# Linear attention with a GeGLU branch on one core: x and v blocks loaded in turn, the gate column made on TensorE, k steps between the weight folds, and the wq transposes released by v

## The chip, the cores and the metric

The kernel runs on one core of one Trainium2 chip. The metric is the device time of one execution in microseconds (us). One execution in each series is profiled; "span" is the length of that execution in its trace, about 2 us below the metric. On one core a run is called "slow" or "fast" by its distance from the fastest run.

## The reference

`x` is 2048 x 640. There are 32 heads of 20 columns. Everything is bf16 with f32 accumulation.

```python
g   = sigmoid((x * gate_w).sum(-1, keepdims=True))
q, k, v = split_heads(x @ wqkv)                       # wqkv 640 x 1920
pq, pk  = q @ w_phi[h], k @ w_phi[h]                  # per head, 20 x 20
phi_q   = concat(softmax(pq), softmax(-pq));  phi_k likewise
kv, z   = phi_k^T v, sum(phi_k)
o       = (phi_q kv) / (phi_q z + 1e-6)
b       = (gelu(x @ w_gate) * (x @ w_up)) @ w_down    # 640 -> 1728 -> 640
out     = g * (o @ wo) + (1 - g) * b
```

## The kernel before

The per-head product with `w_phi` is folded into the weights: `wk2 = wk . blockdiag(w_phi)` and `wq2` likewise, 640 x 640 each. So the kernel needs `wk^T` and `wq^T`: the first by TensorE transposes of the loaded `wk_raw`, the second by six transposing DMAs. Operations are issued in program order on each engine (`pe`, `act`, `dve`, `pool`) and each DMA on a queue (`sp` or `act`). A helper adds a semaphore wait for every hazard, also for a PSUM bank that is still to be read. There are eight banks; numbers such as `(6, 7)` are banks, and `"a"` or `"d"` says whether ACT or DVE moves the result from PSUM to SBUF (evicts it). In the code below, a tile is 128 rows of `x`; `k_early` makes the k product of one tile and its exponentials (exps) on ACT (`Ek`), `k_norm` normalises them on DVE, `pq` is a product with `wq2` and its exps (`Eq`), and `gram` is the product `phi_k^T v`.

The loads, in the order of issue:

```python
        xload(0, "sp"); xload(2, "act"); xload(1, "sp"); xload(3, "act")    # 128 x 640 each
        for kt in range(KD):                                                # five v blocks
            sc.dma("sp", ... self.wvk[:, kt, 0:D] <- w3[:, kt, 2 * D:3 * D], writes=[("wv", kt)])
        sc.dma("act", ... wphi_sb <- w_phi, "h d f -> d h f", writes=["wphi"])
        sc.dma("sp", ... wk_raw <- w3[:, :, D:2 * D], writes=["wk_raw"])    # 640 x 640 at once
        sc.dma("sp", gload, writes=["wgate"])                               # gate_w as a column
        for g, (h0, nh) in enumerate(self.GH):                              # six transposing DMAs
            sc.dma("sp", lambda e: e.dma_start_transpose(self.wqT[:, g, :], self.wqkv[:, h0*DH:h0*DH+P]),
                   reads=["wk_raw"] if g == 0 else [], writes=[("wqT", g)])
        xblock(1); xblock(2); xblock(3)      # transposing DMAs of the rest of x
        # ... the FFN weights follow
```

One fold makes one 128-row block of `wk2` or `wq2` from six groups of heads. It needs two banks and all six groups of the transposed weight:

```python
    def fold(self, kt, which, banks, ekey):
        for g, (h0, nh) in enumerate(self.GH):
            pe.matmul(bank(banks[h0 // 16])[...], wT[0:rows, g, kt*P:(kt+1)*P], self.BD[...], start=True, stop=True)
        # one eviction of both banks, by DVE or ACT, into wvk[:, kt, D:2D] or wq2[:, kt, :]
```

The order up to the steady loop (the part that the change rewrites):

```python
        for i in range(self.NWARM):                       # 7 matmuls of zeros
            pe.matmul(self.bank(3), self.zero[:, 0:P], self.zero[:, :])
        for t, ek in enumerate("adad"):
            self.x_transpose(t, 4 + t, ek)                # x tiles 0..3 on TensorE
        self.v_first({(1, 3): [lambda: self.blockdiag((6, 7))],      # v of four tiles, kt outermost
                      (4, 0): [ve([0], "a")],
                      (4, 1): [tk(0, 6, "d"), ve([1], "a")],         # tk: wk transposes of one group
                      (4, 2): [tk(1, 7, "d"), ve([2], "a")]})        # ve: eviction of v
        self.w_transposes("k", (2, 3, 4, 5), (0, 6, 7, 0), "dadd")
        # ... evictions of v
        for kt, (bk, ek) in enumerate(zip((6, 1, 4, 6, 0), "adada")):
            self.fold(kt, "k", (bk, bk + 1), ek)
        self.k_early(0, 2)                                # k tile 0: banks 2, 3; then its exps on ACT
        self.k_early(1, 4)
        self.fold(0, "q", (6, 7), "d")
        self.fold(1, "q", (0, 1), "a")
        self.k_early(2, 2)
        self.fold(2, "q", (6, 7), "d")
        self.fold(3, "q", (0, 1), "a")
        self.fold(4, "q", (6, 7), "d")
        self.k_norm(0)
        self.k_early(3, 4)
        self.k_norm(1)
        self.pq(0, 1, 1); self.pq(0, 0, 0); self.pq(0, 3, 3)
        self.gram(0)
        self.k_norm(2); self.pq(0, 2, 2); self.k_norm(3)
        for t in range(4, NT):                            # the steady loop
            self.vk(t)
            # ... k_norm, pq, gram; then the FFN and the output
```

The softmax here doesn't subtract the row's maximum and nothing guards it: scores larger than these inputs give would overflow.

## Time and profile before

| | before |
|---|---|
| time, median of 3 first runs | 307.3 us (306.21 to 307.35) |
| span of the profiled run | 304.7 us |
| TensorE busy | 298.0 us, 98% |
| first 512-column matmul of the steady loop | 30.97 us |
| from there to the start of the last matmul | 270.5 us |

The first two fences are from the page of the kernel before: busy time by engine, TensorE's row of the busy tenths over 40 slices, and the chain that ended last: the last instruction, followed back at each step to what released it.

```profile
PE 298.0 (98%) x2011; PEld 175.3 (58%) x2011; DVE 160.0 (53%) x312; ACT 106.8 (35%) x189; POOL 29.8 (10%) x59
...
PE   7998999999999999999999999999999999999996
```

```profile
PE 94%; DMA 2%; ACT 1%; DVE 1%; issue 0%; SPq 0%; ACTq 0%; DVEq 0%
```

TensorE is the bound, and what is left lies at the start. The chain in order of time (start, length, what) for the kernel before:

```profile
1.72 5.08 DMA wvk<-in_A_wqkv_dram
...
13.62 0.85 PE ps L327 x15
...
14.49 0.49 DVE wkT L334
...
14.99 0.50 DVE wkT L334
...
15.53 0.37 PE ps L345 x4
...
15.90 0.74 ACT wvk L360
...
18.14 2.41 PE ps L365 x17
20.55 0.61 PE ps L345 x12
21.16 1.37 PE ps L365 x10
...
27.09 0.99 ACT Eq L494 x2
...
28.12 1.25 PE ps L488 x5
```

The chain begins with the first v block (landed 6.80), passes the last two evictions of `wkT` (last one done at 15.49), the folds and k tiles 0 and 1 (until 20.55), the first two q folds, k tile 2, and ends its gaps with the eviction before pq(0,3) at 28.12. After that it is TensorE without a break.

### The profile page before, as it was taken

The page shows a single profiled execution, that of the slowest core. Times are in us where ns is not written, and L with a number is a line of the kernel's source. Part 1 is how long each engine was busy: PE and PEld are TensorE (multiplying, and loading weights), DVE is VectorE, ACT ScalarE, POOL GpSimd, SP SyncE. Part 2 cuts the span into 40 slices and gives each one's busy share as a digit, 9 for nine tenths or more (in the row PEclk, how much of TensorE's full clock was granted, in tenths as well). Part 3 has the DMA queues.
Part 4 walks back from the last instruction along what each step waited for, and adds up shares of the span by engine and source line. Part 5 has one row for each costly group of instructions (what it writes and reads, how often), then busy time and mean ns, then how long its engine had stood idle before and what let it go on. Part 6 is the DMA issues. An engine that isn't in the chain of part 4 may idle for free.

```text
span 304.7 us, 5022 instructions
## 1 busy us (share of the span) xinstructions
PE 298.0 (98%) x2011; PEld 175.3 (58%) x2011; DVE 160.0 (53%) x312; ACT 106.8 (35%) x189; POOL 29.8 (10%) x59
## 2 busy tenths in 40 slices
PE   7998999999999999999999999999999999999996
PEld 4664565655555555677545567754457764545763
DVE  1438999586775877234367710435770044567000
ACT  3388666667674222111322211123221122222111
POOL 7100000000000011111011000101110010111000
PEclk9999999999999999999999999999999999999999
DMA  7589996000000011120120111011111001110401
GB/s 222 140 150 209 369 369 221 0 2 0 2 0 0 2 22 24 24 65 25 43 20 4 22 24 43 24 43 23 17 6 44 24 26 41 22 22 0 45 22 45
DMA packets 34641, 18.29 MB, mean 60 GB/s; under 512 B 25850, under 2 KB 34618, under 8 KB 34618
## 3 DMA queue, kind: packets, MB, share of 16 engines
q1 hardware_dynamic: 33680, 17.62, 22.8%
q10 hardware_dynamic: 938, 0.35, 0.4%
q8 instruction: 16, 0.26, 0.4%
q14 instruction: 7, 0.06, 0.1%
HBM read 9.78 MB, written 2.62 MB: 41 GB/s over the span
## 4 chain that ended last, share of the span: by engine, by line
PE 94%; DMA 2%; ACT 1%; DVE 1%; issue 0%; SPq 0%; ACTq 0%; DVEq 0%
PE ps L572 37%; PE ps L654 20%; PE ps L365 12%; PE ps L660 7%; PE ps L488 6%; PE ps L609 4%; PE ps L462 4%; PE ps L376 2%; DMA wvk<-in_A_wqkv_dram 2%; PE ps L582 1%; PE ps L345 1%; ACT Eq L494 1%; PE ps L327 0%; ACT Ek L423 0%; DVE wkT L334 0%
## 5 line engine op out<-in xcount | busy, mean ns | idle before, releaser
L572 PE MATMUL ps<-xT,wu_sb 128*128 128x512 bf16 x260 | 64.6, 379 | 0.2 <-ACT Eq L494 0.2
L572 PE MATMUL ps<-xT,wg_sb 128*128 128x512 bf16 x260 | 64.6, 379 | 0.0
L654 PE MATMUL ps<-wd_sb,hT 128*128 128x320 bf16 (+2 forms) x448 | 63.8, 299 | 0.0
L575 ACT ACTIVATE gl<-ps 128x512 bf16<-128x512 f32 x52 | 31.1, 597 | 83.2 <-PE ps L572 81.0
L577 DVE TENSOR_TENSOR hT<-ps,gl 128x512 bf16<-128x512 f32 x52 | 35.7, 688 | 42.9 <-PE ps L572 42.9
L654 PEld LDWEIGHTS ps<-wd_sb,hT 128*128 128x128 bf16 x448 | 43.1, 98 | 18.2 <-DVE hT L577 0.4
L572 PEld LDWEIGHTS ps<-xT,wu_sb 128*128 128x128 bf16 x260 | 25.4, 98 | 31.1 <-issue 0.7
L365 PE MATMUL ps<-wvk,xT 128*128 128x512 bf16 (+2 forms) x220 | 40.6, 335 | 0.2 <-DVE wvk L358 0.2
L572 PEld LDWEIGHTS ps<-xT,wg_sb 128*128 128x128 bf16 x260 | 24.9, 98 | 26.9
L670 ACT ACTIVATE outsb<-ps,Gm 128x640 bf16<-128x640 f32 (+2 forms) x17 | 13.0, 763 | 74.1 <-PE ps L660 74.1
L638 POOL TENSOR_TENSOR Og<-O_59,O_60 128x640 bf16<-128x640 bf16 x16 | 22.3, 1396 | 167.8 <-DVE O_60 L636 167.8
L365 PEld LDWEIGHTS ps<-wvk,xT 128*128 128x128 bf16 x220 | 21.1, 97 | 19.5 <-DVE wvk L358 0.6
L434 DVE TENSOR_REDUCE Dk<-Ek 128x64 f32<-128x1280 bf16 x16 | 23.7, 1482 | 10.0 <-ACT gcol L426 10.0
L625 DVE RECIPROCAL RH<-ps 128x32 f32<-128x32 f32 x16 | 5.7, 358 | 43.9 <-PE ps L609 42.8
L443 DVE TENSOR_TENSOR Ek<-Ek,Dk 128x640 bf16<-128x640 bf16 x32 | 25.0, 822 | 0.5
L488 PE MATMUL ps<-xT,wq_50 128*128 128x512 bf16 x100 | 24.7, 378 | 0.3 <-ACT Eq L494 0.3
L660 PE MATMUL ps<-wo_sb,goT 128*128 128x320 bf16 (+2 forms) x160 | 24.5, 299 | 0.0
L494 ACT ACTIVATE Eq<-ps 128x512 bf16<-128x512 f32 x40 | 21.8, 607 | 5.4 <-PE ps L488 5.4
L423 ACT ACTIVATE Ek<-ps 128x640 bf16<-128x640 f32 x32 | 20.7, 703 | 2.2 <-PE ps L365 2.2
L660 PEld LDWEIGHTS ps<-wo_sb,goT 128*128 128x128 bf16 x160 | 15.5, 98 | 6.3
L609 PEld LDWEIGHTS ps<-KV,Eq 128*128 128x128 bf16 x192 | 12.0, 98 | 3.1
L609 PE MATMUL ps<-KV,Eq 128*128 128x154 bf16 x192 | 13.7, 221 | 0.0
(68 smaller groups left out, 178.7 us busy)
## 6 DMA issues: line engine op xcount, KB each, us to landing
out_dram<-outsb SPq DMA_DIRECT2D x15, 160.0 KB, 1.8
wd_sb<-in_B_w_down_dram SPq DMA_DIRECT2D x1, 2080.0 KB, 12.7
wg_sb<-in_B_w_gate_dram SPq DMA_DIRECT2D x1, 1120.0 KB, 7.0
wu_sb<-in_B_w_up_dram SPq DMA_DIRECT2D x1, 1120.0 KB, 9.5
wg_sb<-in_B_w_gate_dram SPq DMA_DIRECT2D x1, 960.0 KB, 9.0
wu_sb<-in_B_w_up_dram SPq DMA_DIRECT2D x1, 960.0 KB, 9.4
wvk<-in_A_wqkv_dram SPq DMA_DIRECT2D x5, 160.0 KB, 4.8
wk_raw<-in_A_wqkv_dram SPq DMA_DIRECT2D x1, 800.0 KB, 6.5
```

What stands on the lines that cost most here:

```text
L365: sc.op("pe", lambda e, kt=kt: e.matmul(self.bank(bank)[:, bcol:bcol + n], self.xT[:, kt, t * P:(t + 1) * P], self.wvk[:, kt, c0:c0 + n], ...
L434: sc.op("dve", lambda e: e.tensor_reduce(self.Dk[:, se, 0, :].rearrange("p (s h) -> p s h", h=H), self.Ek[:, se, :, :].rearrange("p s (h d ...
L443: sc.op("dve", lambda e, v=v, r=r: e.tensor_tensor(v, v, r, ALU.mult), reads=[("Rk", se)], writes=[("Ek", se, s)])
L488: sc.op("pe", lambda e, kt=kt: e.matmul(self.bank(bank), self.wq2[:, kt, i * P:(i + 1) * P], self.xT[:, kt, b * self.BT:(b + 1) * self.BT] ...
L494: sc.op("act", lambda e, s=s, scale=scale: e.activation(self.Eq[:, s, i, b * self.BT:(b + 1) * self.BT], self.bank(bank), AF.Exp, scale=sc ...
L572: sc.op("pe", lambda e, kt=kt, w=w, bk=bk: e.matmul(self.bank(bk), w[:, kt, c * P:(c + 1) * P], xs(kt), start=(kt == 0), stop=(kt == self. ...
L575: sc.op("act", lambda e: e.activation(self.gl[:, slot, :], self.bank(banks[0]), AF.Gelu_apprx_tanh), reads=[("ps", banks[0])], writes=[("g ...
L577: sc.op("dve", lambda e: e.tensor_tensor(self.hT[:, c, :], self.bank(banks[1]), self.gl[:, slot, :], ALU.mult), reads=[("ps", banks[1]), ( ...
L609: sc.op("pe", lambda e, s=s, i=i, n=n, o0=o0, k0=k0, bk=bk, r=r: e.matmul(self.bank(bk)[:, o0:o0 + n], self.Eq[:, s, i, t * P:(t + 1) * P] ...
L638: sc.op("pool", lambda e: e.tensor_tensor(self.Og[:, sl, :], self.O1[:, sl, :], self.O2[:, sl, :], ALU.add), reads=[("O", 0, sl), ("O", 1, ...
L654: sc.op("pe", lambda e: e.matmul(self.bank(bk, w), self.hT[:, c, tt * P:(tt + 1) * P], self.wd_sb[:, c, w0:w0 + w], start=(c == 0), stop=F ...
L660: sc.op("pe", lambda e: e.matmul(self.bank(bk, w), self.goT[:, gs, k, :], self.wo_sb[:, k, w0:w0 + w], start=False, stop=(k == self.KD - 1 ...
```

## The change

Its intent is to let TensorE work earlier and to leave it fewer gaps: x and v blocks come in turn, so v steps start before all of x is there; the gate column, a load of 640 single elements, is replaced by a row load and five small matmuls; the k steps of tiles 0 and 1 fill the time in which the folds are evicted; and the wq transposes are issued when v is loaded. The core of the diff, cuts marked:

```diff
-        xload(0, "sp")
-        xload(2, "act")
-        xload(1, "sp")
-        xload(3, "act")
-        for kt in range(KD):
-            sc.dma("sp", lambda e, kt=kt: e.dma_start(self.wvk[:, kt, 0:D], ...), writes=[("wv", kt)])
-        sc.dma("act", ... wphi ...)
+        sc.dma("act", ... self.gw_row[0:1, :] <- gate_w as one row, writes=["gw_row"])
+        for i in range(4):
+            xload(i)            # all on "sp"
+            vload(i)
+        sc.dma("sp", ... wphi ...)
+        vload(4)
         sc.dma("sp", ... wk_raw ...)
-            sc.dma("sp", gload, writes=["wgate"])
         for g, (h0, nh) in enumerate(self.GH):
             sc.dma("sp", ... dma_start_transpose(self.wqT[:, g, :], ...),
-                    reads=["wk_raw"] if g == 0 else [], writes=[("wqT", g)])
+                    reads=[("wv", 4)] if g == 0 else [], writes=[("wqT", g)])
 ...
-        for i in range(self.NWARM):  # 7
-        # four x transposes, v with kt outermost, block diagonal after (kt 1, tile 3)
+        warm(4)
+        self.gate_column(5)     # five 1x128 by 1x1 matmuls, one small copy on DVE
+        warm(1)
+        xt(0, 6, "a")
+        warm(1)
+        xt(1, 7, "d")
+        vs(0, 0); vs(0, 1); vs(1, 0); vs(1, 1)      # v_step(tile, kt)
+        xt(2, 6, "a")
+        vs(0, 2); vs(1, 2)
+        xt(3, 7, "d")
+        # ... the other v steps, block diagonal after vs(2, 0..2), wk transposes as before
-        for kt, (bk, ek) in enumerate(zip((6, 1, 4, 6, 0), "adada")):
-            self.fold(kt, "k", (bk, bk + 1), ek)
-        self.k_early(0, 2)
-        self.k_early(1, 4)
+        self.fold(0, "k", (6, 7), "d")
+        self.fold(1, "k", (4, 5), "a")
+        ks(0, 0); ks(1, 0)                          # k_step(tile, kt); tile t in banks 2t, 2t + 1
+        self.fold(2, "k", (6, 7), "d")
+        ks(0, 1); ks(1, 1)
+        self.fold(3, "k", (4, 5), "a")
+        self.fold(4, "k", (6, 7), "d")
+        ks(0, 2); ks(1, 2); ks(0, 3); ks(1, 3)
+        for t in (0, 1):
+            ks(t, 4)
+            self.k_evac(t, 2 * t)
         self.fold(0, "q", (6, 7), "d")
-        self.fold(1, "q", (0, 1), "a")
-        self.k_early(2, 2)
+        self.fold(1, "q", (4, 5), "d")
+        self.k_early(2, 0)
         self.fold(2, "q", (6, 7), "d")
-        self.fold(3, "q", (0, 1), "a")
-        self.fold(4, "q", (6, 7), "d")
+        self.fold(3, "q", (4, 5), "d")
+        self.fold(4, "q", (6, 7), "a")
         self.k_norm(0)
-        self.k_early(3, 4)
+        self.k_early(3, 2)
```

More of the change, by code (lines that the diff above doesn't have):

```diff
@@ L157, in alloc @@
         self.zero = T("zero", [P, 512], BF16)
+        self.gw_row = T("gw_row", [1, D], BF16)
+        self.one = T("one", [1, 1], BF16)
         self.gcol = T("gcol", [P, NT], F32)
@@ L191, in alloc @@
             [("xtok", [P, self.TB, D], BF16), ("wk_raw", [P, KD, D], BF16),
-             ("wkT", [P, 6, D], BF16), ("wqT", [P, 6, D], BF16), ("wq_raw", [P, KD, D], BF16)],
+             ("wkT", [P, 6, D], BF16), ("wqT", [P, 6, D], BF16)],
             [("goT", [P, 6, KD, P], BF16), ("O1", [P, 2, D], BF16), ("O2", [P, 2, D], BF16),
@@ L208, in loads @@
         w3 = self.wqkv.rearrange("(kt p) n -> p kt n", p=P)
-        def gload(e):
-            with nc.allow_non_contiguous_dma(reason="gate_w as a column"):
-                return e.dma_start(self.wvk[:, :, 2 * D:2 * D + 1], self.gw.rearrange("(kt p o) -> p kt o", p=P, o=1))
-        def xload(t, q):
-            sc.dma(q, lambda e: e.dma_start(self.xtok[:, t, :], self.x[t * P:(t + 1) * P, :]), writes=[("xtok", t)])
-        xload(0, "sp")
-        xload(2, "act")
-        xload(1, "sp")
-        xload(3, "act")
@@ L219, in loads, with xload @@
-        for kt in range(KD):
-            sc.dma("sp", lambda e, kt=kt: e.dma_start(self.wvk[:, kt, 0:D], w3[:, kt, 2 * D:3 * D]), writes=[("wv", kt)])
-        sc.dma("act", lambda e: e.dma_start(self.wphi_sb[:, :].rearrange("d (h f) -> d h f", f=DH),
-                                            self.wphi.rearrange("h d f -> d h f")), writes=["wphi"])
-        sc.dma("sp", lambda e: e.dma_start(self.wk_raw[:, :, :], w3[:, :, D:2 * D]), writes=["wk_raw"])
-        if self.QDMA:
-            sc.dma("sp", gload, writes=["wgate"])
-            for g, (h0, nh) in enumerate(self.GH):
-                sc.dma("sp", lambda e, g=g, h0=h0: e.dma_start_transpose(
-                    self.wqT[:, g, :], self.wqkv[:, h0 * DH:h0 * DH + P]),
-                    reads=["wk_raw"] if g == 0 else [], writes=[("wqT", g)])
-        else:
-            sc.dma("sp", lambda e: e.dma_start(self.wq_raw[:, :, :], w3[:, :, 0:D]), writes=["wq_raw"])
-            sc.dma("sp", gload, writes=["wgate"])
+        def xload(t):
+            sc.dma("sp", lambda e: e.dma_start(self.xtok[:, t, :], self.x[t * P:(t + 1) * P, :]), writes=[("xtok", t)])
@@ new lines, in vload @@
+        def vload(kt):
+            sc.dma("sp", lambda e: e.dma_start(self.wvk[:, kt, 0:D], w3[:, kt, 2 * D:3 * D]), writes=[("wv", kt)])
+        sc.dma("act", lambda e: e.dma_start(self.gw_row[0:1, :], self.gw.rearrange("(o n) -> o n", o=1)), writes=["gw_row"])
+        for i in range(4):
+            xload(i)
+            vload(i)
+        sc.dma("sp", lambda e: e.dma_start(self.wphi_sb[:, :].rearrange("d (h f) -> d h f", f=DH),
+                                           self.wphi.rearrange("h d f -> d h f")), writes=["wphi"])
@@ L234, in xblock @@
+        vload(4)
+        sc.dma("sp", lambda e: e.dma_start(self.wk_raw[:, :, :], w3[:, :, D:2 * D]), writes=["wk_raw"])
+        for g, (h0, nh) in enumerate(self.GH):
+            sc.dma("sp", lambda e, g=g, h0=h0: e.dma_start_transpose(
+                self.wqT[:, g, :], self.wqkv[:, h0 * DH:h0 * DH + P]),
+                reads=[("wv", 4)] if g == 0 else [], writes=[("wqT", g)])
         def xblock(b, after=()):
@@ L237, in xblock @@
                 reads=after, writes=[("xT", t) for t in range(b * 4, b * 4 + 4)])
-        xblock(1, [] if self.QDMA else ["wq_raw"])
+        xblock(1)
         xblock(2)
@@ L317, in blockdiag, with wk_transposes @@
             reads=rd, writes=["BD"])
-    def w_transposes(self, which, gs, banks, ekeys):
+    def wk_transposes(self, gs, banks, ekeys):
         sc = self.sc
-        raw, T = (self.wk_raw, self.wkT) if which == "k" else (self.wq_raw, self.wqT)
         for g, b, ek in zip(gs, banks, ekeys):
@@ L327, in w_transposes, with gate_column @@
                 sc.op("pe", lambda e, kt=kt: e.transpose(
-                    pv[0:rows, kt * P:(kt + 1) * P], raw[:, kt, h0 * self.DH:h0 * self.DH + rows], self.ident[:, :]),
-                    reads=["w%s_raw" % which, "ident"], writes=[("ps", b)], signal=(kt == self.KD - 1))
-            dst = T[0:rows, g, :]
+                    pv[0:rows, kt * P:(kt + 1) * P], self.wk_raw[:, kt, h0 * self.DH:h0 * self.DH + rows],
+                    self.ident[:, :]),
+                    reads=["wk_raw", "ident"], writes=[("ps", b)], signal=(kt == self.KD - 1))
+            dst = self.wkT[0:rows, g, :]
             src = pv[0:rows, 0:self.D]
-            wr = [("w%sT" % which, g)]
             if ek == "d":
-                sc.op("dve", lambda e: e.tensor_copy(dst, src), reads=[("ps", b)], writes=wr)
+                sc.op("dve", lambda e: e.tensor_copy(dst, src), reads=[("ps", b)], writes=[("wkT", g)])
             else:
-                sc.op("act", lambda e: e.activation(dst, src, AF.Copy), reads=[("ps", b)], writes=wr)
+                sc.op("act", lambda e: e.activation(dst, src, AF.Copy), reads=[("ps", b)], writes=[("wkT", g)])
+    def gate_column(self, b):
+        sc = self.sc
+        for kt in range(self.KD):
+            sc.op("pe", lambda e, kt=kt: e.matmul(
+                self.bank(b)[:, kt:kt + 1], self.gw_row[0:1, kt * P:(kt + 1) * P], self.one[0:1, 0:1],
+                start=(kt == 0), stop=(kt == self.KD - 1), skip_group_check=True),
+                reads=["gw_row", "one"], writes=[("ps", b)], signal=(kt == self.KD - 1))
+        sc.op("dve", lambda e: e.tensor_copy(
+            self.wvk[:, :, 2 * self.D:2 * self.D + 1], self.bank(b, self.KD).unsqueeze(2)),
+            reads=[("ps", b)], writes=["wgate"])
     def fold(self, kt, which, banks, ekey):
@@ L369, in proj, with v_step, k_step @@
                 writes=[("ps", bank)], signal=(kt == self.KD - 1))
-    def v_first(self, extra):
+    def v_step(self, t, kt):
         sc = self.sc
-        for kt in range(self.KD):
-            for t in range(4):
-                for c0, n, bk, col in ((0, 480, t, 0), (480, 160, 4 + t // 3, 160 * (t % 3))):
-                    sc.op("pe", lambda e, kt=kt, t=t, c0=c0, n=n, bk=bk, col=col: e.matmul(
-                        self.bank(bk)[:, col:col + n], self.xT[:, kt, t * P:(t + 1) * P], self.wvk[:, kt, c0:c0 + n],
-                        start=(kt == 0 and col == 0), stop=(kt == self.KD - 1), skip_group_check=True),
-                        reads=[("xT", t), ("wv", kt)], writes=[("ps", bk)], signal=(kt == self.KD - 1))
-                for f in extra.get((kt, t), ()):
-                    f()
+        for c0, n, bk, col in ((0, 480, t, 0), (480, 160, 4 + t // 3, 160 * (t % 3))):
+            sc.op("pe", lambda e, c0=c0, n=n, bk=bk, col=col: e.matmul(
+                self.bank(bk)[:, col:col + n], self.xT[:, kt, t * P:(t + 1) * P], self.wvk[:, kt, c0:c0 + n],
+                start=(kt == 0 and col == 0), stop=(kt == self.KD - 1), skip_group_check=True),
+                reads=[("xT", t), ("wv", kt)], writes=[("ps", bk)], signal=(kt == self.KD - 1))
+    def k_step(self, t, kt):
+        sc = self.sc
+        for c0, n, bk, col in ((640, 384, 2 * t, 128), (1024, 257, 2 * t + 1, 0)):
+            sc.op("pe", lambda e, c0=c0, n=n, bk=bk, col=col: e.matmul(
+                self.bank(bk)[:, col:col + n], self.xT[:, kt, t * P:(t + 1) * P], self.wvk[:, kt, c0:c0 + n],
+                start=(kt == 0), stop=(kt == self.KD - 1)),
+                reads=[("xT", t), ("wk2", kt), "wgate"], writes=[("ps", bk)], signal=(kt == self.KD - 1))
     def v_first_evac(self, ts, ek, tail):
@@ L510, in attention_state @@
         order = [(b, i) for b in range(self.NB) for i in range(self.KD)]
-        self.sc.op("dve", lambda e: e.memset(self.zero[:, :], 0.0), writes=["zero"])
-        for i in range(self.NWARM):
-            self.sc.op("pe", lambda e: e.matmul(self.bank(3), self.zero[:, 0:P], self.zero[:, :], start=True, stop=True),
-                       reads=["zero"], writes=[("ps", 3)])
-        for t, ek in enumerate("adad"):
-            self.x_transpose(t, 4 + t, ek)
-        tk = lambda g, b, ek: (lambda: self.w_transposes("k", (g,), (b,), ek))
@@ L518, in attention_state @@
-        ve = lambda ts, ek, tail=False: (lambda: self.v_first_evac(ts, ek, tail))
-        self.v_first({(1, 3): [lambda: self.blockdiag((6, 7))],
-                      (4, 0): [ve([0], "a")],
-                      (4, 1): [tk(0, 6, "d"), ve([1], "a")],
-                      (4, 2): [tk(1, 7, "d"), ve([2], "a")]})
-        self.w_transposes("k", (2, 3, 4, 5), (0, 6, 7, 0), "dadd")
-        ve([0, 1, 2], "a", True)()
-        ve([3], "a")()
-        ve([3], "a", True)()
-        for kt, (bk, ek) in enumerate(zip((6, 1, 4, 6, 0), "adada")):
-            self.fold(kt, "k", (bk, bk + 1), ek)
@@ L529, in attention_state, with warm @@
-        self.k_early(0, 2)
-        self.k_early(1, 4)
+        sc = self.sc
+        sc.op("dve", lambda e: e.memset(self.zero[:, :], 0.0), writes=["zero"])
+        sc.op("dve", lambda e: e.memset(self.one[:, :], 1.0), writes=["one"])
+        def warm(n):
+            for i in range(n):
+                sc.op("pe", lambda e: e.matmul(self.bank(3), self.zero[:, 0:P], self.zero[:, :], start=True, stop=True),
+                      reads=["zero"], writes=[("ps", 3)])
+        vs, ve, xt = self.v_step, self.v_first_evac, self.x_transpose
@@ new lines, in attention_state @@
+        tk = lambda g, b, ek: self.wk_transposes((g,), (b,), ek)
+        warm(4)
[4 more added lines that the diff above has]
+        xt(1, 7, "d")
+        vs(0, 0)
+        vs(0, 1)
+        vs(1, 0)
+        vs(1, 1)
+        xt(2, 6, "a")
+        vs(0, 2)
+        vs(1, 2)
+        xt(3, 7, "d")
+        for kt in range(3):
+            vs(2, kt)
+        self.blockdiag((6, 7))
+        for kt in range(4):
+            vs(3, kt)
+        for t in range(3):
+            vs(t, 3)
@@ new lines, in attention_state @@
+        vs(0, 4)
+        ve([0], "a", False)
+        vs(1, 4)
+        tk(0, 6, "d")
+        ve([1], "a", False)
+        vs(2, 4)
+        tk(1, 7, "d")
+        ve([2], "a", False)
+        vs(3, 4)
+        for g, b, ek in zip((2, 3, 4, 5), (0, 6, 7, 0), "dadd"):
+            tk(g, b, ek)
+        ve([0, 1, 2], "a", True)
+        ve([3], "a", False)
+        ve([3], "a", True)
+        ks = self.k_step
+        self.fold(0, "k", (6, 7), "d")
+        self.fold(1, "k", (4, 5), "a")
+        for t in (0, 1):
+            ks(t, 0)
@@ L531, in attention_state @@
+        self.fold(2, "k", (6, 7), "d")
+        for t in (0, 1):
+            ks(t, 1)
+        self.fold(3, "k", (4, 5), "a")
+        self.fold(4, "k", (6, 7), "d")
+        for kt in (2, 3):
+            for t in (0, 1):
+                ks(t, kt)
+        for t in (0, 1):
+            ks(t, 4)
+            self.k_evac(t, 2 * t)
         self.fold(0, "q", (6, 7), "d")
-        self.fold(1, "q", (0, 1), "a")
-        self.k_early(2, 2)
+        self.fold(1, "q", (4, 5), "d")
+        self.k_early(2, 0)
@@ L595, in num @@
         DB, DH = self.DB, self.DH
-        old = [("xtok", k) for k in range(4)] + ["wk_raw"] + [("wkT", g) for g in range(6)] + [("wqT", g) for g in range(6)] + ["wq_raw"]
+        old = [("xtok", k) for k in range(4)] + ["wk_raw"] + [("wkT", g) for g in range(6)] + [("wqT", g) for g in range(6)]
         parts = {0: [(0, 0, 6), (1, 6, 12), (2, 12, 15)], 1: [(2, 16, 19), (3, 19, 25), (4, 25, 31)]}
@@ L686 @@
     NUMB = 2
-    NWARM = 7
-    QDMA = True
     oldw = [(w, k) for w in ("wv", "wk2", "wq2") for k in range(5)] + ["wgate"]
```

## The prediction

> **What bounds the kernel.** TensorE: the page gives PE 298.0 of 304.7 us busy and 94% of the chain of waits. From 28.1 us on that chain is practically PE alone, and the change leaves this part's order as it is. Only the first 28 us can pay. There the chain (in order of time) is DMA until 6.80 us (last part of the first v block), then PE with holes: two wkT evictions on DVE at 14.5 (1.0), fold evictions at 15.9 and 17.2 (partly filled), a q-fold eviction at 22.8 (0.9), and exps of k tile 3 plus Eq at 25.7 (PE idle 0.3). PE's own work up to 31.1 us, where the steady loop starts, sums to about 22.4 us: x transposes 1.1, v 5.4, block diagonal 0.4, wk transposes 1.7, folds 3.0, k tiles 5.5, pq 4.3, gram 0.7. The first x lands at 3.9. Even a perfect start gives under 5 us, 1.6%.
>
> **Removed, added, moved.**
> 1. Loads. Before, x lands at 3.9 to 4.8, v at 6.8 to 8.3, wk at 10.6; blocks of one queue follow each other by 0.45 us. In turn: x0 about 3.5, v0 4.0, x1 4.4, v1 4.9, v3 6.7, wphi 8.2, v4 8.6, wk 10.6 to 11 (same bytes). wphi's short rows no longer sit beside v. The Trainium skill (DMA: Bandwidth & Descriptors, "Issuing engines are not separate DMA queues") says that DMAs from several engines share 16 engines and interleave; the 2 us between first and last part of v0, while wphi ran, agrees.
> 2. PE starts v at about 5.5 instead of 6.93, partly at the half clock: the clock record turns full at 5.90. The skill (TensorE: Matmul & The Clock Gate, Part 1) says the clock opens after about 3.4 us of sustained work, in a varying phase; I expect about 6 again. By 6.8 four of twenty v steps (0.27 each) are done, but two x transposes (0.56) are open: gain 0.5 to 0.8. v is then PE-bound. Last wkT eviction about 14.8, not 15.49.
> 3. Gate column: five tiny matmuls, one small DVE copy, in place of two warm-up matmuls: free. Its old DMA (landed 11.1) was not waited for: no gain.
> 4. wq transposes 2 us earlier: before, PE did not wait for them: no gain. Behind wk on the same queue they should delay it by under 0.5.
> 5. k behind the fold: only two bank pairs; with k steps between, PE waits about 0.9 us from last wkT eviction to end of k tile 1, as before: 5.0 against 5.06. But both k tiles end 0.27 us apart, so their exps (1.36 each) queue; k tile 2 reuses tile 0's banks and waits about 0.6, tile 3's exps come later, and pq(0,3) starts 8.1 us after k tile 1 instead of 7.6: loss about 0.5.
>
> **Sum.** -0.7 (start) +0.0 (fold/k) +0.5 (exps, banks) = -0.2 us, all on the critical path; the intent may pay a little better than my hand schedule, so -0.6. Predicted 306.7 us, 8 in 10 between 305.2 and 308.0. Faster by over 2%: 0.02; within 2%: 0.96; slower: 0.02.
>
> **What would show it.** First v matmul at 5.3 to 5.8; last x transposed near 7.9; last wkT eviction 14.5 to 15; a PE wait on ACT Ek before k tile 2; the first 512-column v/k matmul of the steady loop at 30 to 31 (before 30.97); from there to the end 273.7 us as before.
>
> **What would make it wrong.** gw_row landing late and holding PE; the clock opening at 7 to 9 us because warm-up has gaps; wphi late, stalling the block diagonal; wq transposes delaying wk to 12 us; or k steps hiding the fold evictions fully (up to 1 us more).

## The result, and the profile after

| | before | after |
|---|---|---|
| time, median of 4 runs | 307.15 us (306.21 to 307.35) | 307.61 us (307.35 to 307.92) |
| span of the profiled run | 304.7 us | 306.1 us |
| TensorE clock full from | 5.90 us | 7.12 us |
| last part of wk landed | 10.61 us | 12.74 us |
| last wkT eviction done | 15.48 us | 15.96 us |
| first 512-column matmul of the steady loop | 30.97 us | 32.54 us |
| from there to the start of the last matmul | 270.5 us | 270.5 us |

The ratio is 1.0021, with a 95% interval of 0.9998 to 1.0044: the same within 2%, and rather slower than faster. All ratios here are the mean time of one kernel's fast runs over the mean of the other's fast runs of the same rounds, so they are not quite the ratios of the medians.

From the page of the kernel after, the lines that answer to those of before:

```profile
PE 297.7 (97%) x1989; PEld 175.2 (57%) x2015; DVE 161.6 (53%) x316; ACT 105.8 (35%) x187; POOL 29.8 (10%) x59
...
PE   8988999999999999999999999999999999999996
```

```profile
PE 91%; DMA 2%; SPq 2%; ACT 1%; DVE 1%; issue 1%; ACTq 0%; DVEq 0%
```

And its chain in order of time:

```profile
5.23 0.84 SPq L216
...
6.11 6.64 DMA wk_raw<-in_A_wqkv_dram
...
15.47 0.50 DVE wkT L329
...
16.01 0.22 PE ps L351
...
16.33 0.84 DVE wvk L364
...
17.21 0.72 PE ps L388 x4
...
18.33 0.83 DVE wvk L364
...
19.21 0.46 PE ps L351 x6
19.67 1.45 PE ps L388 x10
...
21.80 0.70 ACT Ek L433
22.50 0.07 ACT gcol L436
22.57 1.52 PE ps L371 x10
...
28.65 0.99 ACT Eq L504 x2
...
29.69 1.25 PE ps L498 x5
```

The chain no longer starts at v: it runs through the queue of issues on SP and then the load of wk, which was issued at 6.11 instead of 4.10 and landed at 12.74. Then it passes DVE evictions of folds 0 and 2 (`wvk L364`), each of which holds TensorE, and the exps of k tile 0 (`Ek`) that k tile 2 must wait for. The first v matmul did come early, at 5.34 us instead of 6.93, but partly before the clock record turned full: its first eight took almost as long as sixteen in the kernel before. The first v matmuls of before and after, from the timelines (start, length, idle time before them):

```profile
6.93 2.34 PE L376 MATMUL ps<-wvk,xT 128*128 128x480 bf16 x16 [0.62 <-DMA wvk<-in_A_wqkv_dram]
...
5.34 2.13 PE L380 MATMUL ps<-wvk,xT 128*128 128x480 bf16 x8
```

The page's busy TensorE time hardly moved (297.7 against 298.0), which says nothing either way: the Trainium skill (Trainium Kernel Development and Optimization, "Performance Expectations") warns that matmul busy time is a bad metric for the distance to a kernel's limit, because matmuls are pipelined. This pair can't test that, because the trace of the changed kernel lacks 26 matmul records (1989 beside 2015 weight loads); its second trace, after_again, has all 2015 and shows 298.7.

Three marks in the trace cut the time into pieces. S1 is from the start to the end of the last `wkT` eviction; S2 from there to the first matmul of the steady loop; the rest is 270.5 us to the start of the last matmul in every trace (270.51 to 270.52). Behind that start come 3.21 to 3.23 us in the traces with the start of before and 3.05 to 3.16 in those with the changed start; why is open. So each kernel's difference is S1 plus S2, less about 0.15 us at the end with the changed start. In the first two traces S1 grew by 0.5 and S2 by 1.1.

### The profile page after: what moved, and what is told of

Its sections match the earlier page's. It is cut to its first block, busy times and chain, and to the rows that moved or that the text cites. A ratio compares the mean times of both kernels' runs of the same rounds, so it can differ in the third digit from the quotient of the medians.

```text
span 306.1 us, 5005 instructions
## 1 busy us (share of the span) xinstructions
PE 297.7 (97%) x1989; PEld 175.2 (57%) x2015; DVE 161.6 (53%) x316; ACT 105.8 (35%) x187; POOL 29.8 (10%) x59
## 4 chain that ended last, share of the span: by engine, by line
PE 91%; DMA 2%; SPq 2%; ACT 1%; DVE 1%; issue 1%; ACTq 0%; DVEq 0%
PE ps L623 36%; PE ps L705 20%; PE ps L371 12%; PE ps L711 7%; PE ps L498 6%; PE ps L660 4%; PE ps L472 4%; DMA wk_raw<-in_A_wqkv_dram 2%; PE ps L633 1%; SPq L216 1%; ACT Ek L433 1%; PE ps L388 1%; SPq L213 1%; PE ps L351 1%; DVE wvk L364 1%
## 5 line engine op out<-in xcount | busy, mean ns | idle before, releaser
L623 PE MATMUL ps<-xT,wg_sb 128*128 128x512 bf16 x251 | 62.8, 379 | 0.3
L371 PE MATMUL ps<-wvk,xT 128*128 128x512 bf16 (+2 forms) x200 | 37.5, 339 | 0.7 <-ACT gcol L436 0.6
L371 PEld LDWEIGHTS ps<-wvk,xT 128*128 128x128 bf16 x200 | 19.3, 97 | 19.1 <-ACT Ek L433 0.7
L444 DVE TENSOR_REDUCE Dk<-Ek 128x64 f32<-128x1280 bf16 x16 | 23.7, 1482 | 10.6 <-ACT gcol L436 10.6
L498 PE MATMUL ps<-xT,wq_50 128*128 128x512 bf16 x91 | 23.4, 378 | 0.8 <-ACT Eq L504 0.3
L711 PEld LDWEIGHTS ps<-wo_sb,goT 128*128 128x128 bf16 x160 | 15.5, 98 | 6.3
```

The costliest lines, as they stand in the source:

```text
L371: sc.op("pe", lambda e, kt=kt: e.matmul(self.bank(bank)[:, bcol:bcol + n], self.xT[:, kt, t * P:(t + 1) * P], self.wvk[:, kt, c0:c0 + n], ...
L444: sc.op("dve", lambda e: e.tensor_reduce(self.Dk[:, se, 0, :].rearrange("p (s h) -> p s h", h=H), self.Ek[:, se, :, :].rearrange("p s (h d ...
L498: sc.op("pe", lambda e, kt=kt: e.matmul(self.bank(bank), self.wq2[:, kt, i * P:(i + 1) * P], self.xT[:, kt, b * self.BT:(b + 1) * self.BT] ...
L623: sc.op("pe", lambda e, kt=kt, w=w, bk=bk: e.matmul(self.bank(bk), w[:, kt, c * P:(c + 1) * P], xs(kt), start=(kt == 0), stop=(kt == self. ...
L711: sc.op("pe", lambda e: e.matmul(self.bank(bk, w), self.goT[:, gs, k, :], self.wo_sb[:, k, w0:w0 + w], start=False, stop=(k == self.KD - 1 ...
```

## The experiments

All twelve runs gave correct results. Each series had five or more runs of each kernel and its own runs of the kernel before on the same chip. Times are compared within a series.

The table collects what the traces (one for each run) show; "old" and "new" name which version of a part is in the kernel. "wk" and "wqT" are the landings of the last parts, "clock" the time from which the record of TensorE's clock is full (before it, in the trace of the changed kernel, five x transposes took 0.74 us, after it 0.44). All are us.

```
trace             loads        wq transposes   k order    clock   wk     S1     wqT    S2     ratio to before (95%)
before            old          after wk        old         5.90  10.61  15.48  20.61  15.49   -
before_again      old          after wk        old         4.98  11.11  15.79  21.53  16.09  0.9994 (0.9972 to 1.0015)
early_tr_before   old          after v         old         6.42  10.79  15.09  18.48  15.47  0.9972 (0.9960 to 0.9985)
new_k_only        old          after wk        new         6.24  11.07  14.85  20.91  16.58  1.0003 (0.9991 to 1.0016)
after             new          after v         new         7.12  12.74  15.96  19.11  16.58  1.0021 (0.9998 to 1.0044)
after_again       new          after v         new         6.27  12.42  15.64  19.08  16.58  1.0014 (1.0000 to 1.0028)
late_tr           new          after wk        new         7.39  12.16  15.65  22.11  16.81  1.0031 (1.0012 to 1.0050)
old_k             new          after v         old         7.32  11.89  15.54  19.27  15.46  0.9985 (0.9972 to 0.9999)
tile0_first       new          after v         new, tile 0 4.88  11.98  15.20  18.63  16.57  1.0007 (0.9987 to 1.0027)
one_tile          new          after v         one tile    4.84  12.37  15.58  19.27  15.75  0.9970 (0.9957 to 0.9984)
old_loads         old (+gw)    after v         new        10.34  11.06  17.45  19.51  16.57  1.0048 (1.0021 to 1.0074)
two_queues        x|v queues   after v         one tile    8.20  11.46  16.36  19.24  15.76  1.0043 (1.0019 to 1.0067)
mix1              old          after wk        old, moved  6.04  10.66  14.66  21.07  16.82  0.9991 (0.9971 to 1.0010)
mix2              old          after v         old, moved  6.88  11.23  15.22  19.12  15.36  0.9962 (0.9949 to 0.9974)
```

The first theory was the prediction's: the new start roughly breaks even and the loss lies in the exps and banks behind the folds. The rival was that the start carries the loss, by accident of a late clock and a late wk.

### after_again: the changed kernel, unaltered

> The changed kernel, unaltered, as a control on this chip and for a second trace. First theory (the loss is in the exps and banks behind the fold, the start only breaks even): 0.1 to 0.5% slower than before, and in the trace about 8.5 us from the end of k tile 1 to pq(0,3) as in the first trace (before 7.6). Rival (the loss of the first trace is the accident of a late wk part and a late clock): last wk part at 10.6 to 11.2 us and clock open near 6 us this time, and time equal to or below before.

Measured: 307.36 us against 306.95, ratio 1.0014. The clock opened at 6.27 this time, and wk still landed at 12.42. S2 was 16.58 again, to the digit. From the end of k tile 1 to pq(0,3) it was 8.3 us, as in the first trace of the changed kernel (8.3) and not quite the 8.5 expected. So the late wk is no accident, and the loss in S2 is fixed.

### new_k_only and old_k: the k order apart from the start

new_k_only is the kernel before with the lines from `self.fold(0, "k", (6, 7), "d")` to `self.k_early(3, 2)` of the diff above; old_k is the changed kernel with those lines taken back.

> Before, with only the fold, k and q-fold order of the changed kernel (banks, evicting engines). First theory: slower than before by 0.7 to 1.2 us (0.25 to 0.4%), all of it between the last wkT eviction and pq(0,3). Rival (the start carries the loss): within 0.3 us of before.

> The changed kernel with the fold, k and q-fold order of before; its new start stays. First theory: 0.7 to 1.2 us faster than the changed kernel, so level with before or up to 0.7 us faster. Rival (the start carries the loss): as slow as the changed kernel.

Measured: new_k_only 307.02 against 306.95, ratio 1.0003; old_k 306.56, ratio 0.9985. The two disagree at first sight. Taking the new k order out of the changed kernel gains 0.8 us (307.36 to 306.56, same series), as the first theory says; putting it into the kernel before costs only 0.07 us. Yet the traces show the same 1.1 us in both places: S2 is 16.58 with the new order and 15.46 to 15.49 with the old. Something in the kernel before must hide the loss when it runs in its usual way. The next series showed what.

### before_again: the kernel before, unaltered

> Before, unaltered: the noise of the comparison, and a second trace of before. Expected: ratio within 0.1% of 1. If the fold, k and q part of a kernel takes the same time in every execution, it is 15.5 us from the last wkT eviction to the first 512-column matmul of the steady loop (first trace 15.49) and 270.5 us from there to the last matmul; all spread of the times must then be in the start, whose last wkT eviction should lie between 15.4 and 16.4.

Measured: 307.49 against 307.24, ratio 0.9994. The expectation failed in one point: S2 was 16.09, not 15.5. The chain in order of time for this run shows why:

```profile
4.11 7.00 DMA wk_raw<-in_A_wqkv_dram
...
11.13 1.23 SPq L227
...
18.65 2.88 DMA wqT<-in_A_wqkv_dram
...
21.57 0.50 PE ps L345 x7
22.07 1.37 PE ps L365 x10
```

Here the first 21.5 us of the chain are not TensorE at all. They are the issues of the earlier loads, wk, then six transposing DMAs issued one after another on SP (`SPq L227`, 1.2 to 1.3 us each, 2.3 in one case), then the landing of the last one, which the first q fold (`L345`) needs. TensorE's waits in the first 32 us of this run (total us, times, longest) list it; those of the first trace of before do not:

```profile
PEld ps L345 <- DMA wqT<-in_A_wqkv_dram: 0.6, 1, 0.6
```

In every trace with transposes that wait for wk, the last one lands 9.8 to 10.4 us after wk. In the first trace of before it landed at 20.61, while the q fold had started at 20.4 and needs the last group last: no wait was recorded, but no slack was left either. So the kernel before has two chains that end within a few tenths of a microsecond of each other. A slower k order can hide behind the second; a faster start would be lost in it. The trace of new_k_only shows the hiding: TensorE waited 0.6 us for wqT there, and none of its waits for `Ek` is listed, yet S2 is the same 16.58 as in the changed kernel, which waits 0.7 us for `Ek` and not for wqT.

### early_tr_before: the wq transposes alone

```diff
-                    reads=["wk_raw"] if g == 0 else [], writes=[("wqT", g)])
+                    reads=[("wv", 4)] if g == 0 else [], writes=[("wqT", g)])
```

> Before, with one line of the change alone: the first wq transpose waits for v, not for wk. If wk plus six serial transposes is a second chain that often ends last before the first q fold (second trace of before: last one landed at 21.5 us, PE waited 0.6 us): last wq transpose at 19 to 19.8 us, no wait for it, 15.5 us from the last wkT eviction to the steady loop in the trace, and 0.2 to 0.7 us faster than before. If PE does not wait for it, as the prediction said: within 0.15 us of before.

Measured: 306.50 us against 307.36, ratio 0.9972: 0.86 us faster (0.46 to 1.23 by the interval of the ratio), a little more than expected. S2 is 15.47, the last transpose lands at 18.48 (expected 19 to 19.8), and TensorE's waits no longer list wqT. All five spans (304.3 to 304.7) lie below all nine of before (305.0 to 305.9). The theory that the wq transposes were a second chain holds, and the claim that they gain nothing falls. The waits for wqT that are seen in the two traces of before (none and 0.6) are shorter than 0.86, so the size of this gain is less sure than its presence. The chain of this run is TensorE work and evictions all the way from 5 us:

```profile
17.75 2.41 PE ps L365 x17
20.16 0.58 PE ps L345 x12
20.74 1.37 PE ps L365 x10
```

### late_tr: the wq transposes put back in the changed kernel

```diff
-                reads=[("wv", 4)] if g == 0 else [], writes=[("wqT", g)])
+                reads=["wk_raw"] if g == 0 else [], writes=[("wqT", g)])
```

> The changed kernel, with the first wq transpose waiting for wk again, not for v. If the early transposes hold up wk: last wk part 1 us or more earlier (11.7 or below) and 0.4 to 1 us faster than the changed kernel. If wk is late from its own causes (issued 2 us later, some engines behind) and the transposes are the ones that wait: last wk part still 12 us or later, time within 0.3 us of the changed kernel.

Measured: 307.98 us, ratio 1.0031, slower than the changed kernel in the same series by 0.6 us of the medians; neither expectation had that. wk landed at 12.16 without any transpose in its way, so the early transposes are not what makes wk late. The Trainium skill (DMA: Bandwidth & Descriptors, "Queues, rings and completion order") says that each DMA engine takes the descriptors of a queue in ring order, though a later one may finish first. The traces with early transposes behind wk agree with the order: the first transpose, issued before wk had landed, landed 0.7 to 1.2 us after it in each (13.47 against 12.74 in the changed kernel). Put back, they landed at 22.11 and cost 0.2 us in this run's S2; the rest of the 0.6 is not seen in the trace.

### old_loads: the loads of before in the changed kernel

```diff
-        for i in range(4):
-            xload(i)
-            vload(i)
-        sc.dma("sp", ... wphi ...)
-        vload(4)
+        xload(0); xload(2, "act"); xload(1); xload(3, "act")
+        for kt in range(KD):
+            vload(kt)
+        sc.dma("act", ... wphi ...)
```

> The changed kernel, with x, v and wphi loaded as before (two queues, v behind x); gate row, early wq transposes and the new orders on the engines stay. If loading in turn is what makes wk late and pays little: last wk part back at 10.6 to 11.3 us, the wait for wk gone, last wkT eviction at 14.8 to 15.3, and 0.3 to 0.8 us faster than the changed kernel. If loading in turn pays: first v matmul back at 6.2 to 6.9 and 0.3 us or more slower than the changed kernel.

Measured: 309.39 us, ratio 1.0048. By its numbers the second expectation is met (first v matmul at 6.48, and slower than the changed kernel by about 0.8 to 1 us, with the changed kernel's ratios of 1.0014 and 1.0021 from other series). But wk did come back to 11.06, as the first theory said, and TensorE could not use it: its clock opened only at 10.34. Matmuls by start, length and idle time before them, from the timeline of this run:

```profile
4.66 0.74 PE L289 MATMUL ps<-ident,xtok 128*128 128x128 bf16 x5
6.48 2.29 PE L382 MATMUL ps<-wvk,xT 128*128 128x480 bf16 x8 [1.08 <-DMA wvk<-in_A_wqkv_dram]
8.57 0.74 PE L289 MATMUL ps<-ident,xtok 128*128 128x128 bf16 x5
```

The new order has only six warm-up matmuls and two x transposes ahead of v; with v landing as before, TensorE stood still for 1.1 us and then did its v steps at half speed (eight matmuls in 2.29 us; the same kind took 2.34 us for sixteen before). The unprofiled spans of this kernel fall into two groups, 305.9 to 306.0 and 307.4 to 307.7. The Trainium skill (TensorE: Matmul & The Clock Gate, Part 1) says that the clock opens after about 3.4 us of sustained work, that the window is free-running, and that it varies from run to run. The trace agrees in kind: where TensorE was fed from 1.26 us on, the clock opened between 4.84 and 7.39 in twelve traces; in the two kernels with a larger gap before the clock was open it opened at 8.20 and 10.34. So this run does not measure the load order alone. That the gap caused the late clock is what the two runs suggest; it was not tested by itself.

### tile0_first: k tile 0 finished before tile 1

```diff
-        for kt in (2, 3):
-            for t in (0, 1):
-                ks(t, kt)
-        for t in (0, 1):
-            ks(t, 4)
-            self.k_evac(t, 2 * t)
+        for t in (0, 1):
+            for kt in (2, 3, 4):
+                ks(t, kt)
+            self.k_evac(t, 2 * t)
```

> The changed kernel, with the last three steps of k tile 0 done before those of k tile 1, so that tile 0's exps start about 0.8 us before tile 1 is done. If the exps of tiles that end together, and the reuse of tile 0's banks, are the loss: the wait before k tile 2 falls from 0.85 to 0.1 to 0.4 us and the time by 0.4 to 0.7 us against the changed kernel. If that wait is not what the time hangs on: within 0.2 us of the changed kernel.

Measured: 307.83 us, ratio 1.0007, and S2 16.57, unchanged. The wait of TensorE's weight loads for ACT Ek did fall from 0.7 us (after_again, first line) to 0.2 (this run, second line), but nothing was gained in S2:

```profile
PEld ps L371 <- ACT Ek L433: 0.7, 1, 0.7
...
PEld ps L371 <- ACT Ek L433: 0.2, 1, 0.2
```

The chain of this run shows three DVE evictions in a row of dependences where the changed kernel had two:

```profile
15.57 0.83 DVE wvk L364
...
16.45 0.72 PE ps L388 x4
17.17 0.30 PE ps L351 x6
...
17.56 0.83 DVE wvk L364
...
18.45 0.47 PE ps L351 x6
...
19.01 0.84 DVE wvk L364
...
19.90 1.27 PE ps L388 x8
```

Folds 0, 2 and 4 all use banks 6 and 7 and all are evicted by DVE: fold 2 is issued behind k steps that need fold 0's eviction, fold 4 waits for fold 2's eviction, and the last step of k tile 0 waits for fold 4's. The exps of tile 0 begin 5.24 us after the last wkT eviction here and 5.24 in the changed kernel. So the queue of exps, which the prediction blamed, is only the place where the delay is seen. The first theory falls in this form. The new theory: two k tiles hold four banks from the first k step on, so the folds are left with two pairs and run through them one after another.

### one_tile: one k tile between the folds

```diff
         self.fold(0, "k", (6, 7), "d")
         self.fold(1, "k", (4, 5), "a")
-        ks(0, 0); ks(1, 0)
-        self.fold(2, "k", (6, 7), "d")
-        ks(0, 1); ks(1, 1)
-        self.fold(3, "k", (4, 5), "a")
-        self.fold(4, "k", (6, 7), "d")
-        # ... remaining steps of both tiles
+        self.fold(2, "k", (2, 3), "d")
+        ks(0, 0)
+        self.fold(3, "k", (6, 7), "a")
+        ks(0, 1)
+        self.fold(4, "k", (4, 5), "d")
+        ks(0, 2); ks(0, 3); ks(0, 4)
+        self.k_evac(0, 0)
+        for kt in range(5):
+            ks(1, kt)
+        self.k_evac(1, 2)
```

> The changed kernel, with only k tile 0 put between the folds, three bank pairs for the folds, evictions split over DVE and ACT, and k tile 1 whole behind them. If the loss of the new k order is the shortage of banks (two k tiles hold four banks, so every second fold waits for a DVE eviction of the same pair): 15.2 to 15.8 us from the last wkT eviction to the steady loop, not 16.6, and 0.7 to 1.2 us faster than the changed kernel. If it is something else that comes with k steps between folds: 16.3 us or more, and level with the changed kernel.

Measured: 306.37 us against 307.36, ratio 0.9970. S2 is 15.75, within the range expected. Against the changed kernel this is 0.44% (0.9970 over 1.0014, two series on two chips, so not a direct comparison), or about 1.3 us, a little more than the 0.7 to 1.2 expected; S2 accounts for 0.8 of it. In its chain one DVE eviction of a fold is left between the wkT eviction and the q folds, where the changed kernel has two and tile0_first three:

```profile
18.25 0.83 DVE wvk L364
...
19.13 1.81 PE ps L388 x12
20.94 0.58 PE ps L351 x12
```

This kernel keeps the k steps between folds and loses nothing by it. So the loss came with the banks and evictions of this particular arrangement, not with the idea. The edit changes pairs, evicting engines and the number of tiles together; which of them counts most stays open. It also gains nothing over the old order (15.75 against 15.47).

### two_queues: x and v side by side

```diff
-            sc.dma("sp", lambda e: e.dma_start(self.xtok[:, t, :], ...), writes=[("xtok", t)])
+            sc.dma("act", lambda e: e.dma_start(self.xtok[:, t, :], ...), writes=[("xtok", t)])
```

(on one_tile)

> The kernel with one k tile between the folds, with the x blocks issued from ACT and the v blocks from SP, so that both are issued side by side and wk is issued about 1.9 us earlier; nothing else differs. If wk was late because ten loads were issued one after the other on one queue: last wk part at 10.6 to 11.3 us (12.37 with one queue), last wkT eviction 0.5 to 1 us earlier and the time 0.3 to 0.8 us below the one-queue version (about 305.7, if the reference stands at 307.2). If taking x and v in turn itself makes the transfers slower: last wk part at 11.8 us or later and time within 0.2 us of the one-queue version.

Measured: 308.40 us against 307.25, ratio 1.0043, slower. wk was issued at 4.20 and landed at 11.46, between the two expectations, so issue explains more than half of its delay against before, but not all. x now stood behind the gate row on ACT's queue: the first block landed at 4.45 instead of 3.14 and the last at 9.00 instead of 7.26. TensorE was idle for 0.6 us before 4.5 us and its clock opened at 8.20. Both expectations for the time failed. The run does not give a version with both an early x and an early wk.

### mix1 and mix2: a version drawn from the traces

mix1 is before, with the wk transposes spread between the v steps of kt 3 and 4, and k tile 3 ahead of the last q fold. mix2 adds the early wq transposes and moves the last q fold:

```diff
-                      (4, 0): [ve([0], "a")],
-                      (4, 1): [tk(0, 6, "d"), ve([1], "a")],
-                      (4, 2): [tk(1, 7, "d"), ve([2], "a")]})
-        self.w_transposes("k", (2, 3, 4, 5), (0, 6, 7, 0), "dadd")
+                      (3, 1): [tk(0, 6, "d")], (3, 2): [tk(1, 7, "a")], (3, 3): [tk(2, 6, "d")],
+                      (4, 0): [tk(3, 7, "d"), ve([0], "a")],
+                      (4, 1): [tk(4, 6, "d"), ve([1], "a")],
+                      (4, 2): [tk(5, 7, "d"), ve([2], "a")]})
 ... mix1
+        self.k_early(3, 4)
         self.fold(4, "q", (6, 7), "d")
-        self.k_early(3, 4)
 ... mix2 instead of these lines, and wq transposes after v
-        self.fold(3, "q", (0, 1), "a")
+        self.fold(3, "q", (0, 1), "d")
+        self.proj(3, 640, 384, 4, 128, ["wk2"])          # first half of k tile 3
+        self.fold(4, "q", (2, 3), "d")
+        self.proj(3, 1024, 257, 5, 0, ["wk2", "wgate"])  # second half
+        self.k_evac(3, 4)
 ...
-        self.pq(0, 3, 3)
+        self.pq(0, 3, 3, 2)                              # in bank 2
```

> Before, with two moves that the traces suggest: the wk transposes spread between the v steps as soon as wk is there, so that their evictions run beside v; and k tile 3 ahead of the last q fold, so that PE has work while DVE evicts a q fold. If the chain before the steady loop is what counts: 1 to 2 us faster than before (0.3 to 0.6%), first matmul of the steady loop at 29 to 30 us. If other waits take their place: within 0.5 us.

> The mixed kernel of the last series, now with the early wq transposes of the change, the last q fold in the middle of k tile 3 and in other banks, and one pq in a bank of its own. If the wq transposes were what the first mixed kernel ended on: no wait for them, steady loop at 29.2 to 30.2 us, 1 to 2 us (0.35 to 0.65%) faster than before. If the moves only trade waits: within 0.5 us of before.

Measured: mix1 307.21 against 307.24, ratio 0.9991, no gain. Its S1 was the shortest of all, 14.66, but its S2 was 16.82, with a wait for the wq transposes (from TensorE's waits in the first 32 us of this run; total us, times, longest):

```profile
PEld ps L345 <- DMA wqT<-in_A_wqkv_dram: 1.0, 1, 1.0
```

A wait of 1.2 us for DVE's eviction of the last q fold, ahead of a `pq`, is on the same list.

mix2, without that wait: 306.08 us against 307.36, ratio 0.9962, the lowest ratio and about 0.5% below the changed kernel's (across series). Its interval overlaps those of early_tr_before (0.9972) and one_tile (0.9970) in the same series, so a gain of its moves beyond the early wq transposes is not shown. It missed its range for the start of the steady loop (30.58, expected 29.2 to 30.2), and its gain of 0.38% lies at the low end of the 0.35 to 0.65% expected. In its chain the last wait has moved to the normalisation of k tile 0 on DVE, ahead of the first gram:

```profile
28.13 0.83 DVE Ek L443
...
29.01 0.65 PE ps L462 x9
```

## Why the prediction was right or wrong

The range held (307.61 in 305.2 to 308.0), and so did "within 2%", the bound (under 5 us to be had, all before the steady loop), and the unchanged rest from the loop to the end (273.7 us foretold, 273.6 measured). The start of the loop was missed: 32.54 and 32.22 us, not 30 to 31. The point, 306.7, was 0.9 us low and on the wrong side of before; 0.4 us of it was an allowance for the intent without a mechanism. The sum was "-0.7 (start) +0.0 (fold/k) +0.5 (exps, banks)". The runs put these terms in its place:

- **Start, -0.7: failed.** First v matmul at 5.3 to 5.8 was right (5.34), but the last wkT eviction was not at 14.5 to 15. Six traces with the new loads and start (after, after_again, late_tr, old_k, tile0_first, one_tile) have S1 of 15.20 to 15.96, mean 15.60; the four with the old ones and the same wk transposes (before, before_again, early_tr_before, new_k_only) 14.85 to 15.79, mean 15.30. So it is about +0.3; the two ranges overlap, but no gain of 0.7 is in them. Two steps failed. The first is "wk 10.6 to 11 (same bytes)": wk landed at 11.89 to 12.74 in those six and at 10.61 to 11.11 in those four, and TensorE waited for it in four of the six (0.3, 0.3, 0.4 and 0.8 us). Same bytes do not mean same time. Ten loads issued one after the other on one queue put the issue of wk at 5.7 to 6.1 instead of 4.1 us, and the 1280-byte packets between 2.7 and 13 us took 66 to 67 ns in the mean (some 1,630 of them in each trace) instead of 60 to 62. two_queues and old_loads, with wk issued at 4.2, brought the landing to 11.46 and 11.06. The prediction had named a wk at 12 us as a danger, but from the wq transposes, which late_tr clears. The second is that early v work counts in full, with the clock "about 6" again. Less the wait for wk, S1 in the six is still 14.8 us where the clock came at 4.84 and 4.88, and 15.3 to 15.7 where it came at 6.27 to 7.39: v steps started early ran in part on a clock not yet full. That the clock sets this part is read from six traces, not tested. In the four old starts S1 follows another thing, the landing of the first v block (5.98 to 7.11 us), by 8.7 to 8.9 us.
- **Fold and k, +0.0, and exps and banks, +0.5: mis-sized.** S2 grew by 1.1, in each of the traces with the new order and early transposes. From the last wkT eviction to the end of k tile 1 it took 5.4 us, not 5.0 (before 5.1), so about +0.3 in place of +0.0; from there to pq(0,3) 8.3 us, not 8.1 (before 7.6), so about +0.75 in place of +0.5. The wait before k tile 2 was foreseen (0.6; seen at 0.6 to 0.7). Its cause was not: tile0_first cut the wait from 0.7 to 0.2 and gained nothing, and one_tile, with a third bank pair and evictions split over both engines, took back 0.8 of the 1.1.
- **"4. wq transposes ... before, PE did not wait for them: no gain": failed.** That line alone gains 0.86 us (early_tr_before). The first trace had shown no wait, because the last transpose landed at 20.61 just as the first q fold came to need it. The landing time was on record, and its slack was not worked out.
- **"they should delay it by under 0.5"** is not contradicted: late_tr landed wk at 12.16, the early ones at 11.89 to 12.74, which is too wide to show less.
- **Gate column, free:** five matmuls took 0.29 us and gw_row landed at 2.54 (2.1 in other runs), just before TensorE needed it. No run measured it by itself.

Together: +0.3 (S1) +1.1 (S2) -0.15 (the end) -0.86 (wq transposes no longer waited for) = +0.4 us, an estimate from means of single traces and one difference of medians, each unsure by some tenths; the two measured differences of the changed kernel are +0.46 and +0.41 us of the medians. The prediction's net effect came out near zero as foretold, but by luck, out of other parts: one part of the change was worth almost a microsecond and two others spent it.

## What to carry to other kernels

No recorded wait is not the same as slack: for every load of a tuned start, note when it lands and when its reader gets there, because two chains that end together hide each other's gains and losses. When parts of a change do not add up (here new_k_only and old_k), look for the second chain before doubting the measurement. Before putting work between evictions, count the banks that this work holds, because the evictions then have fewer to rotate through.

## What the Trainium skill lacked or had wrong

- TensorE: Matmul & The Clock Gate, Part 1: it gives the transition at around 4 us into sustained matmul activity, plus or minus 0.5 us from run to run. Here, with TensorE fed from 1.26 us by matmuls and transposes with short pauses, the clock opened 3.6 to 6.1 us after the first matmul (4.84 to 7.39 on the trace's scale), and 6.9 and 9.1 us after it where there was one larger gap. The spread of the twelve traces is 2.5 us, where this sentence of the page allows 1.
- DMA: Bandwidth & Descriptors, "Issuing engines are not separate DMA queues": it says that several engines only save the time to initiate a DMA, usually small beside the DMA. In these starts that time was not small: 0.4 to 0.5 us for most 160 KB loads, whose landings in the trace of before lay 0.2 to 0.45 us apart (v blocks), so the one-queue order issued wk 1.6 to 2.0 us later.
- The same page has no time for issuing larger transposing DMAs on this chip. The runs show 1.2 to 1.3 us on SP for most 640 x 128 blocks of wq (up to 2.5), 2.5 to 3.6 us for 512 x 640 of x, and 9.8 to 11.0 us from the first issue of six of the first kind to the last landing.
- No page that I used says anything of packets that slow down with the order of the same loads: here 66 to 67 ns for 1280 bytes with x and v in turn on one queue, 60 to 62 with x first or with x and v on two queues. The cause is open.
